# The reciprocal of two pairs in the slot of an existing small tile (linear attention and a squared-ReLU feed-forward, one core)

## The chip, the cores and the metric

One NeuronCore of one Trainium2 chip. The metric is the device time of one execution in microseconds (us). A shorter time is better.

## The reference

Eight batches, eight heads, 576 positions, 64 channels per head. Every head goes through a linear attention, the eight heads are laid side by side to 512 channels, and the 4608 rows go through a feed-forward of width 2048:

```python
q_s = softmax(q, over the 64 channels)
k_s = softmax(k, over the 576 positions)
kv  = einsum('bhsd,bhse->bhde', k_s, v)
x   = einsum('bhsd,bhde->bhse', q_s, kv)      # then heads side by side: 4608 x 512
h   = x @ w_in                                # 512 x 2048
out = (relu(h) ** 2) @ w_out                  # 2048 x 512
```

## The kernel before

**Numbers.** Everything is float32. A large matrix product is made from three products of `float32r` operands: each operand is split into a high part and a low rest, and high by high, high by low and low by high are added up in one PSUM bank.

**Stages.** The rows are worked in blocks of 512 columns (one block per batch, and one block of the eight batches' last 64 positions). Blocks 0, 1 and 2 go through the feed-forward one by one: `h_part` (lines 894 to 899) multiplies a 128x128 piece of `wi[fc]` (stationary operand) with a 512-column piece of `x_hi` or `x_lo` (moving operand), 12 matmuls for each of 16 chunks `fc`; `relu`, `square`, `g_high` and `g_low` make `g_hi` and `g_lo`; `out_part` multiplies pieces of them (stationary) with the 512 columns of `wo[fc]` (moving), 12 matmuls a chunk. Blocks 0 and 2 read `x_hi0` and `x_lo0`, block 1 reads `x_hi1` and `x_lo1`. The other six blocks are worked in three steps of two blocks with a Strassen-like scheme, seven products for eight: `product` multiplies a piece of a weight tile `wp` (stationary) with 512 columns of `xh_...` or `xl_...` (moving), and `out_unit` multiplies a piece of `g` (stationary) with the 512 columns of `wp`, `wo` or `wo_back` (moving). Attention of later batches runs between the matmuls of earlier blocks.

**Order.** Two lists written by hand, `ORDER` and `LIST`, give the order of all units; `InOrder` ties each instruction to the one before it on its engine, so that every engine issues in just that order. SyncE issues nearly all DMAs, also in that order. What an instruction waits for follows from the tiles that it reads and writes.

**The reciprocals.** `kv` of a pair of heads has 128 rows and a 65th column with the sum that the rows are divided by. `rs` adds 1e-9 to that column and `rr` takes the reciprocal, on VectorE, into a tile `rs` of 128x1 with the tag `rs0` or `rs1`. From batch 2 on, two pairs are taken together (`joint`): there `kr` does the same for two columns at once in a tile `rsj` of 128x2 with a tag of its own, and multiplies with it into `kf`.

**Where tiles lie.** SBUF is laid out by pool in the order `const`, `work`, `attn`, `weights`, `stay`, and behind them `first` and later `late`; within a pool, tags lie in the order in which they are first used, each slot rounded up to 32 bytes. Adding up the sizes (the first tile of `const` starts at byte 1152 of a partition) gives these starts:

| tiles | pool | first byte | modulo 64 |
|---|---|---|---|
| `x_hi0`, `x_lo0`; in the same slots later `g` | const | 1152, 9344 | 0 |
| a tile of 352 bytes that nothing uses (`pad_back`) | const | 37152 | 32 |
| `r`, `w_sum`, `c`, `g_hi`, `g_lo` | work | 37504 to 47744, 2048 apart | 0 |
| `mc0`, `mc1`, `rs0`, `rs1` | attn | 61056, 61088, 61120, 61152 | 0, 32, 0, 32 |
| `rsj`, the last tile of its pool | attn | 63104 | 0 |
| `w`, `a`, `T`, `tb`, `xf`, `o`, `left` | weights | 63136 to 76960 | 32 |
| `wi`, `wo`, `wp`, `xh_...`, `xl_...`, `far` | stay | 79520 and on, 4096 apart | 32 |
| `x_hi1`, `x_lo1`; in the same slots later `wo_back`; `kvs` | late | 210592, 218784, 226976 | 32 |

The pieces that a matmul reads of these tiles begin a multiple of 512 bytes behind the tile's start, so a piece has the tile's remainder modulo 64.

Of the kernel before, what the change touches and what calls it, by code (L numbers as in the profile page):

```python
# [8 lines left out]
F32 = mybir.dt.float32  # L9
# [7 lines left out]
P = 128  # L17
# [10 lines left out]
NB = 2  # L28
# [281 lines left out]
def attention_ffn_kernel(ctx: ExitStack, tc: tile.TileContext, q, k, v, w_in, w_out, out):  # L310
# [14 lines left out]
    attn_pool = ctx.enter_context(tc.tile_pool(name="attn", bufs=1))  # L325
# [23 lines left out]
    def next_bank(who):  # L349
        if who == "z":  # L350
            return rest[2]
        n = taken[who]
        taken[who] += 1
        return rest[n % 2 + (0 if who == "h" else 2)]
# [12 lines left out]
    for tag in ("m0", "m1"):  # L367
        attn_pool.tile([P, 2, D], F32, name=tag, tag=tag)
    for tag in ("mc0", "mc1", "rs0", "rs1"):
        attn_pool.tile([P, 1], F32, name=tag, tag=tag)  # L370

    v0 = [t.rearrange("p h j d -> p (h j d)")[:, : 2 * LOW * D].rearrange("p (h j d) -> p h j d", h=2, j=LOW) for t in vt]

# [93 lines left out]
    def pair_units(b, pr):  # L467
        n = b * NPAIR + pr
        i = n % NB
# [4 lines left out]
        s = {}  # L474
# [64 lines left out]
            e.pool.memset(vt[pr][:, :, :, D:], 1.0)  # L539

        def rs():
            s["rs"] = attn_pool.tile([P, 1], F32, name="rs", tag=f"rs{i}")
            e.dve.tensor_scalar_add(s["rs"], s["kv"][:, D : D + 1], 1e-9)

        def rr():
# [46 lines left out]
        for f in (  # L592
            kmax, T, mc, spread, ke, kexp, qm, qsub, qexp, qs, qadd, rc, qmul, kv, padv, rs, rr, kvn_,
            qt4, cp, qt1, cps, at, xhi, xlo, atl, left, XL,
        ):
            units[f"{f.__name__.rstrip('_')}{b}{pr}"] = f

    def attention(b, pr, two):
        n = b * NPAIR + pr
        kk, qq, vv = tiles(b, pr)  # L600
        st = {"v": vv}
# [92 lines left out]
                    )  # L694

        def rs():
            st["rs"] = attn_pool.tile([P, 1], F32, name="rs", tag=f"rs{n % NB}")
            e.dve.tensor_scalar_add(st["rs"], st["kv"][:, D : D + 1], 1e-9)

        def rr():  # L700
# [114 lines left out]
        def keep_raw():  # L815
            e.sp.dma_start(x_raw[b][pr // 2][:, pr % 2], st["xr"])

        fine = dict(Bw=bounce_out, B=bounce_in, rs=rs, rr=rr, kf=kf, kh=kv_high, kl=kv_low)
        fine.update(
            kmax=lambda: (k_max(), k_rows(), k_spread()), ke=k_sub, kexp=k_exp, qsub=lambda: (q_max(), q_less()),  # L820
            qexp=q_exp, qn=lambda: (q_sum(), q_scale(), q_turn()), kv=kv, qh=q_high, ql=q_low,
        )
        micro = dict(
            km=k_max, k1=k_rows, k2=k_spread, ke=k_sub, kx=k_exp, qm=q_max, qd=q_less, qx=q_exp, qs=q_sum, qy=q_scale,
            tb=q_turn, Bw=bounce_out, B=bounce_in, kp=k_pad, kr=lambda: (rs(), rr(), kf()),
            kh=kv_high, kl=kv_low, XL=keep_left, XR=keep_raw, kvat=kv, st=st,
            kv=lambda: kv(next_bank("z" if b > THREE[-1] else "a")[:, : D + 1]),
# [22 lines left out]
    def joint(b, pr):  # L850
        sts = [pairs[b, pr + i]["st"] for i in range(NB)]
        st = {}

        def kv():
            ps = st["kv"] = next_bank("z" if b > THREE[-1] else "a")[:, : NB * P].rearrange("p (i f) -> p i f", i=NB)
            for i in range(NB):
                pairs[b, pr + i]["kvat"](ps[:, i, : D + 1])

        def kr():
            rs = attn_pool.tile([P, NB, 1], F32, name="rsj", tag="rsj")  # L860
            e.dve.tensor_scalar_add(rs, st["kv"][:, :, D : D + 1], 1e-9)
            e.dve.reciprocal(rs, rs)
            st["kf"] = attn_pool.tile([P, NB, D], F32, name="kf", tag="kf0")
            e.dve.tensor_tensor(st["kf"], st["kv"][:, :, :D], rs.broadcast_to([P, NB, D]), op=ALU.mult)

        def kz():
            z = kv_split[0].bitcast(F32)
            if b in THREE:
                e.pool.memset(z[HALF:, :, :, :D], 0.0)
                e.pool.memset(z[:HALF, :, :, D:], 0.0)  # L870
            else:
                e.pool.memset(z[HALF:, :, 0, D:], 0.0)
                e.pool.memset(z[:HALF, :, 1, D:], 0.0)

        def kh():
            kvs, kf = kv_split[0], st["kf"]
            for h in range(2):
                e.act.copy(kvs[half[h], :, 0, half[h]] if b in THREE else kvs[half[h], :, h, :D], kf[half[h]])
            if b not in THREE:
                for h in range(2):  # L880
                    e.act.copy(kvs[half[1 - h], :, h, :D], kf[half[h]])

        def kl():
            kvs, kf = kv_split[0], st["kf"]
            for h in range(2):
                own = half[h]
                lo, hi = (kvs[own, :, 1, own], kvs[own, :, 0, own]) if b in THREE else (
                    kvs[own, :, h, D:], kvs[own, :, h, :D]
                )
                e.dve.tensor_tensor(lo, kf[own], hi.bitcast(F32), op=ALU.subtract)  # L890

        return dict(kv=kv, kr=kr, kz=kz, kh=kh, kl=kl)

    def h_part(ps, blk, fc, cc):
# [78 lines left out]
    for j in range(NPR + 1):  # L973
        for p in PAIR if j < NPR else TAIL:
            i = j - (p in ("S4", "o1"))
# [261 lines left out]
    for token in ORDER:  # L1237
        name, _, bank = token.partition(":")
# [98 lines left out]
```

## Time and profile before

| | |
|---|---|
| median of 3 runs | 851.17 us (850.32 to 852.03) |
| the profiled execution | 850.77 us, span in the profile 849.0 us |
| TensorE busy | 840.7 us, 99% of the span |
| VectorE, ScalarE, GpSimd busy | 538.4, 487.2, 288.1 us |
| granted TensorE clock, mean over the span | 1.00 |

The span runs from the first to the last instruction in the trace; the profiled execution's own time is 1.77 us longer. PE is TensorE's matmul, PEld its load of the stationary operand, DVE VectorE, ACT ScalarE, POOL GpSimd, SP SyncE. All of the kernel's instructions are recorded by one helper and so bear one line number, L290; they are told apart by the tiles (`out<-in`, buffer numbers left out). A matmul's duration in the trace overlaps with that of the next one; how fast a row of matmuls goes is read from the starts: the start of one group less the start of the group before it, divided by the number of matmuls in the latter. Below, this is called the pitch.

### The profile page before, as it was taken

What the parts mean: (1) busy time and instruction counts of PE and PEld (TensorE: products, weight loads), DVE (VectorE), ACT (ScalarE), POOL (GpSimd) and SP (SyncE); (2) the same over time, 40 slices, a digit from 0 to 9 for tenths busy, and PEclk for the clock granted to TensorE, in tenths of its full rate; (3) what the DMA queues carried; (4) which work ended last, traced back from release to release, by engine and by line L of the source; (5) the groups of instructions that cost most, each with busy time, mean ns of one, the idle gap of its engine ahead of it and who ended that gap; (6) DMA issues with size and microseconds to landing.
All of it is one profiled execution on the core that took longest, in us unless ns stands there. A gap on an engine that the chain in (4) does not pass through costs nothing.

```text
span 849.0 us, 12969 instructions
## 1 busy us (share of the span) xinstructions
PE 840.7 (99%) x4286; PEld 678.0 (80%) x4286; DVE 538.4 (63%) x1098; ACT 487.2 (57%) x898; POOL 288.1 (34%) x269
## 2 busy tenths in 40 slices
PE   8999999999999999999999999999999999999997
PEld 6777788888888887888888878888888788888886
DVE  7898888778787779857677787553257132222421
ACT  4888866667556656676567455565473144444411
POOL 4578654466657546242323252211004000000000
PEclk9999999999999999999999999999999999999999
DMA  9969987963787889989889847866575275554611
GB/s 239 277 184 298 278 281 223 311 196 103 220 263 225 234 264 268 277 271 252 239 245 265 258 140 213 266 188 179 170 237 170 93 225 162 155 169 152 178 48 49
DMA packets 156594, 179.65 MB, mean 212 GB/s; under 512 B 51696, under 2 KB 120304, under 8 KB 156528
## 3 DMA queue, kind: packets, MB, share of 16 engines
q1 hardware_dynamic: 155776, 177.88, 70.6%
q10 hardware_dynamic: 752, 0.95, 0.4%
q8 instruction: 34, 0.56, 0.3%
q14 instruction: 32, 0.26, 0.1%
HBM read 133.69 MB, written 45.09 MB: 211 GB/s over the span
## 4 chain that ended last, share of the span: by engine, by line
PE 90%; DVE 3%; DMA 3%; issue 1%; SPq 1%; ACT 1%; POOL 1%; DVEq 0%; POOLq 0%; ACTq 0%
PE bank L290 90%; DMA raw_o<-in_moe_w_out_dram 1%; DVE m L290 1%; DMA qt<-in_q_dram 1%; DMA kt<-in_k_dram 1%; SPq L290 1%; DMA raw_i<-in_moe_w_in_dram 0%; POOL qs L290 0%; DVE g_lo L290 0%; DVE bank L290 0%; DVE w L290 0%; DVE ke L290 0%; DVE xf L290 0%; DVE qs L290 0%; DVE qm L290 0%
## 5 line engine op out<-in xcount | busy, mean ns | idle before, releaser
L290 PE MATMUL bank<-wp,g 128*128 128x512 f32 x648 | 164.7, 395 | 0.0
L290 PEld LDWEIGHTS bank<-wp,g 128*128 128x128 f32 x648 | 120.5, 187 | 28.6
L290 PE MATMUL bank<-x_hi,wi 128*128 128x512 f32 x384 | 132.9, 400 | 0.0
L290 PE MATMUL bank<-xh_T,wp 128*128 128x512 f32 x384 | 131.4, 392 | 0.0
L290 PE MATMUL bank<-wo,g_hi 128*128 128x512 f32 x384 | 122.3, 399 | 0.0
L290 PE MATMUL bank<-xh_B,wp 128*128 128x512 f32 x288 | 98.4, 392 | 0.0
L290 POOL TENSOR_TENSOR qs<-qT,qs 64x640 fp32r<-64x640 f32 (+1 forms) x40 | 64.2, 1606 | 95.1 <-ACT qs L290 66.1
L290 DVE TENSOR_TENSOR c<-c,bank 128x512 f32<-128x512 f32 x48 | 32.9, 686 | 89.5 <-ACT c L290 89.1
L290 PEld LDWEIGHTS bank<-x_hi,wi 128*128 128x128 f32 x384 | 72.2, 188 | 17.2 <-issue 0.5
L290 PEld LDWEIGHTS bank<-xh_T,wp 128*128 128x128 f32 x384 | 72.1, 188 | 17.0 <-ACT bank L290 1.2
L290 ACT ACTIVATE far<-far 128x512 f32<-128x512 f32 x96 | 60.7, 632 | 40.3 <-DVE far L290 39.0
L290 PEld LDWEIGHTS bank<-wo,g_hi 128*128 128x128 f32 x384 | 70.5, 188 | 16.6 <-issue 0.7
L290 PE MATMUL bank<-wo,g_lo 128*128 128x512 f32 x192 | 75.8, 395 | 0.0
L290 PE MATMUL bank<-x_lo,wi 128*128 128x512 f32 x192 | 75.5, 393 | 0.0
L290 PE MATMUL bank<-xl_T,wp 128*128 128x512 f32 x192 | 74.7, 389 | 0.0
L290 PE MATMUL bank<-wo_back,g 128*128 128x512 f32 x288 | 73.2, 395 | 0.0
L290 DVE TENSOR_TENSOR far<-far,bank 128x512 f32<-128x512 f32 x48 | 32.9, 686 | 50.4 <-PE bank L290 50.3
L290 DVE TENSOR_TENSOR g<-far,g 128x512 fp32r<-128x512 f32 x48 | 33.9, 745 | 48.2 <-ACT g L290 48.1
L290 PEld LDWEIGHTS bank<-wo_back,g 128*128 128x128 f32 x288 | 53.6, 187 | 12.7
L290 PEld LDWEIGHTS bank<-xh_B,wp 128*128 128x128 f32 x288 | 54.1, 188 | 11.7
L290 POOL TENSOR_TENSOR qn<-qn,qs 128x640 f32<-128x640 f32 x30 | 37.8, 1262 | 72.4 <-DVE qs L290 56.2
L290 ACT CAST g<-far 128x512 fp32r<-128x512 f32 x48 | 27.6, 620 | 54.1 <-PE bank L290 53.9
(138 smaller groups left out, 1525.3 us busy)
## 6 DMA issues: line engine op xcount, KB each, us to landing
wp<-w_outs SPq DMA_DIRECT2D x54, 512.0 KB, 4.4
wp<-w_sums SPq DMA_DIRECT2D x96, 256.0 KB, 3.7
wp<-w_own SPq DMA_DIRECT2D x72, 256.0 KB, 3.5
out_dram<-o SPq DMA_DIRECT2D x68, 128.0 KB, 2.8
raw_i<-in_moe_w_in_dram SPq DMA_DIRECT2D x16, 512.0 KB, 6.6
raw_o<-in_moe_w_out_dram SPq DMA_DIRECT2D x16, 512.0 KB, 6.8
bounce<-tb SPq DMA_DIRECT2D x24, 320.0 KB, 3.4
qT<-bounce SPq DMA_DIRECT2D x96, 80.0 KB, 3.0
```

What stands on the lines that cost most here:

```text
L290: ins = f(*args, **kwargs)
```

## The change

The tile `rsj` is gone. `kr` takes the tag `rs0`, whose slot now has room for two columns; the single reciprocals `rs` take the first column of a tile of that size. All instructions, their order and their shapes stay as they were. A slot of 8 bytes is rounded up to 32 like one of 4, so `rs0` and `rs1` keep their places and sizes; the slot of `rsj` at the end of the pool `attn` is no longer there, and everything in `weights`, `stay`, `first` and `late` starts 32 bytes lower.

```diff
     for tag in ("mc0", "mc1", "rs0", "rs1"):
-        attn_pool.tile([P, 1], F32, name=tag, tag=tag)
+        attn_pool.tile([P, NB if tag[0] == "r" else 1], F32, name=tag, tag=tag)
...
         def rs():
-            s["rs"] = attn_pool.tile([P, 1], F32, name="rs", tag=f"rs{i}")
+            s["rs"] = attn_pool.tile([P, NB], F32, name="rs", tag=f"rs{i}")[:, :1]
             e.dve.tensor_scalar_add(s["rs"], s["kv"][:, D : D + 1], 1e-9)
...
         def rs():
-            st["rs"] = attn_pool.tile([P, 1], F32, name="rs", tag=f"rs{n % NB}")
+            st["rs"] = attn_pool.tile([P, NB], F32, name="rs", tag=f"rs{n % NB}")[:, :1]
             e.dve.tensor_scalar_add(st["rs"], st["kv"][:, D : D + 1], 1e-9)
...
         def kr():
-            rs = attn_pool.tile([P, NB, 1], F32, name="rsj", tag="rsj")
+            rs = attn_pool.tile([P, NB], F32, name="rs", tag="rs0").rearrange("p (i o) -> p i o", o=1)
             e.dve.tensor_scalar_add(rs, st["kv"][:, :, D : D + 1], 1e-9)
             e.dve.reciprocal(rs, rs)
```

## Rows read from the trace of the kernel before

**Rows 1.** Page: span, and busy time of TensorE.

```profile
span 849.0 us, 12969 instructions
PE 840.7 (99%) x4286; PEld 678.0 (80%) x4286; DVE 538.4 (63%) x1098; ACT 487.2 (57%) x898; POOL 288.1 (34%) x269
```

**Rows 2.** Chain in order of time: start us, length us, what.

```profile
46.49 116.16 PE bank L290 x591
...
162.73 0.60 ACT g_hi L290
...
195.48 648.72 PE bank L290 x3178
```

**Rows 3.** Tile rsj: duration ns min/median/max, first and last start us.

```profile
L290 DVE RECIPROCAL rsj<-rsj x11: 165/166/167, 173.9 to 561.7; 128x2 f32<-128x2 f32 x11
```

**Rows 4.** Timeline of TensorE at 700 us: start us, length us, what.

```profile
701.31 2.96 PE L290 MATMUL bank<-wp,g 128*128 128x512 f32 x12
704.11 0.39 PE L290 MATMUL bank<-xh_B,wp 128*128 128x512 f32 x1
...
706.60 0.40 PE L290 MATMUL bank<-xh_B,wp 128*128 128x512 f32 x1
706.84 0.86 PE L290 MATMUL bank<-wo_back,g 128*128 128x512 f32 x3
```

**Rows 5.** Groups on the page: the load of the stationary operand.

```profile
L290 PEld LDWEIGHTS bank<-wp,g 128*128 128x128 f32 x648 | 120.5, 187 | 28.6
```

**Rows 6.** Timeline of TensorE from 805 us.

```profile
804.84 2.96 PE L290 MATMUL bank<-wp,g 128*128 128x512 f32 x12
...
841.24 2.95 PE L290 MATMUL bank<-wp,g 128*128 128x512 f32 x12
```

**Rows 7.** Timeline of TensorE: a chunk of block 1, then one of block 2.

```profile
212.87 0.40 PE L290 MATMUL bank<-x_hi,wi 128*128 128x512 f32 x1
...
215.63 0.63 PE L290 MATMUL bank<-wo,g_hi 128*128 128x512 f32 x2
...
294.74 0.40 PE L290 MATMUL bank<-x_hi,wi 128*128 128x512 f32 x1
...
297.54 0.60 PE L290 MATMUL bank<-qs,kvs 128*128 128x320 f32 x3
```

**Rows 8.** Timeline of TensorE: warm-up matmuls (two looks, which overlap).

```profile
6.15 3.82 PE L290 MATMUL bank<-x_hi 128*128 128x512 f32 x16
...
8.22 1.52 PE L290 MATMUL bank<-x_hi 128*128 128x512 f32 x6
```

**Rows 9.** Windows: busy PE, PEld, DVE, ACT, POOL (instructions), PE clock, DMA share, GB/s.

```profile
7.10:9.50 2.40, 2.40 (x12) 2.00 (x11) 2.33 (x3) 0.85 (x2) 2.26 (x2) 1.00 1.05 292
325.00:450.00 125.00, 125.00 (x654) 101.96 (x653) 93.50 (x218) 83.46 (x152) 46.55 (x37) 1.00 0.90 257
450.00:849.00 399.00, 394.19 (x1781) 319.54 (x1779) 178.27 (x315) 184.81 (x323) 45.06 (x33) 1.00 0.57 174
805.00:840.00 35.00, 35.00 (x151) 28.11 (x151) 7.76 (x12) 6.88 (x12) 0.00 (x0) 1.00 0.13 42
```

**Rows 10.** Windows, TensorE alone, by tile: wi, g_hi, g_lo, g, wp; last g again.

```profile
46.49:849.00 802.51, 132.67 (x525) 1.00 0.70 209
46.49:849.00 802.51, 122.29 (x384) 1.00 0.70 209
46.49:849.00 802.51, 75.80 (x192) 1.00 0.70 209
46.49:849.00 802.51, 286.21 (x1152) 1.00 0.70 209
46.49:849.00 802.51, 397.19 (x1656) 1.00 0.70 209
450.00:849.00 399.00, 243.52 (x990) 1.00 0.57 174
```

**Rows 11.** Waits of SyncE's DMA queue: us in total, times, longest us.

```profile
SPq L290 <- PE bank L290: 218.7, 120, 5.2
```

## The prediction

> **What bounds the kernel now.** I read the page first. TensorE is busy for 99% of the span [rows 1], so the next view is the chain of waits in order of time: two pieces on TensorE hold 116.16 and 648.72 us of the 849.0 us, and only the first 46.5 us and the stretch from 162.73 to 195.48 us run over other engines and loads [rows 2]. Even there TensorE is hardly ever without work. A change that leaves every instruction and its order alone can then matter in one way: by what one matmul takes. So the third view is TensorE's timeline, and what to take from it is the pitch, not the printed length of a matmul (0.39 or 0.40 us, which overlaps with the next).
>
> Near 700 us the pitch has two levels. Twelve matmuls with `wp` stationary and `xh_B` or `xl_B` moving run from 704.11 to 706.84 us: 2.73 us / 12 = 227.5 ns. The twelve before them, with `g` stationary and `wp` moving, run from 701.31 to 704.11 us: 2.80 / 12 = 233.3 ns [rows 4]. All have 512 columns of float32r, at a granted clock of 1.00, its 2.4 GHz level [rows 9]. The load of the next stationary operand (187 ns [rows 5]) runs beside the matmul before it, so each matmul has two reads of SBUF under way: its moving columns and the next stationary piece.
>
> What tells the two kinds apart in the table of addresses: `wp` and `xh_B` both start at 32 modulo 64, while `g` starts at 0 and `wp` at 32. I test this reading in three places:
> - Traffic does not make it. From 804.84 to 841.24 us thirteen chunks of 12 with `g` stationary take 36.40 us / 156 = 233.3 ns [rows 6], though DMA is at 0.13 and GpSimd idle there [rows 9]. Near 700 us, with far more going on, it is the same number.
> - The same code at another address differs. A chunk `h` of block 1 (moving `x_hi1` at 32, stationary `wi` at 32) takes 215.63 - 212.87 = 2.76 us / 12 = 230.0 ns; one of block 2 (moving `x_hi0` at 0, stationary `wi` at 32) takes 297.54 - 294.74 = 2.80 / 12 = 233.3 ns [rows 7].
> - Only the warm-up has both operands at 0 (both are `x_hi0`): sixteen matmuls from 6.15 us have 3.82 less the 0.39 of the last = 3.43 us / 15 = 228.7 ns, and the last six 1.13 / 5 = 226 ns [rows 8], while DMA is at 1.05 of its engines and VectorE busy nearly throughout [rows 9].
>
> So I read: **unequal remainders modulo 64 cost 233.3 ns, equal ones about 227.5.** The rows speak of 64 only because no pair differs otherwise.
>
> **The change part by part.**
> - *The slot.* The table's last tile of `attn` (32 bytes) goes, so `weights`, `stay` and `late` go from 32 to 0 modulo 64, while `const` and `work` stay at 0. All large matmuls then have both operands at 0.
> - *kr.* The same add, reciprocal (165 ns [rows 3]) and multiply on the same shapes: 0. Sharing `rs0` could add a wait on its earlier readers. Those on ScalarE belong to batches 0 and 1 and come before every joint in the order; later ones are on VectorE, as `kr` itself. Should one wait appear, the copies `kvs` stand behind it, and VectorE's own slack (538.4 of 849.0 us busy [rows 1]) covers it.
> - *Matmuls that go from unequal to equal remainders.* From 46.49 us on: 384 with `g_hi`, 192 with `g_lo`, 1152 with `g`, and of 525 with `wi` all but block 1's 16 x 12 = 192, so 333 [rows 10]. Together 2061.
>   - The 1152 of the three steps: 1152 x (233.3 - 227.5) = 6.7 us.
>   - The other 909 lie before 325 us, where equal pairs run at 230.0 (block 1) rather than 227.5. Bounds: 909 x 3.3 = 3.0 and 909 x 5.8 = 5.3 us; I take 4.1, the middle, since the warm-up's 228.7 lies between the two.
> - *Matmuls that stay equal* (from 32 and 32 to 0 and 0): 1656 - 648 = 1008 products [rows 5, 10] and block 1's 192. I take 0. Upper bound on the cost if 0 and 0 means the 228.7 of the warm-up's sixteen: 1008 x 1.2 = 1.2 us.
> - *The first 46.5 us*: the chain there runs over loads and VectorE, 0.
> - *162.73 to 195.48 us*: the chain is not on TensorE; a faster TensorE waits for ScalarE, VectorE and GpSimd instead. Its share of the gain, 32.75 / 802.5 x 10.8 = 0.4 us, I take off.
> - *Transfers into moved tiles.* No row has one transfer at both addresses. SyncE's queue waited 218.7 us for TensorE [rows 11], so refills follow TensorE rather than lead it: 0 from both sides, within the range.
>
> Sum: 6.7 + 4.1 - 0.4 = 10.4 us. The profiled execution's 850.77 us become 840.4 (span 838.6); the median shown is 0.4 above it, so **840.8 us**. What ends last stays TensorE. Next in line is DMA at 0.90 between 325 and 450 us [rows 9].
>
> The far ends: all 2061 at 226 ns give 2061 x 7.3 = 15.0 us, so 836.2. All large matmuls at 228.7 give 2061 x 4.6 - 1.2 = 8.3 us, so 842.9.
>
> **A rule against it.** The rows show the pitch of one matmul to go with the addresses of two operands [rows 4, 7]. The Trainium skill, "TensorE: Matmul & The Clock Gate", section "Step-by-step: what each phase is for", says that TensorE has two independent read ports in SBUF and that loading the next weights takes no read bandwidth from the running matmul. By that rule an address could not matter and the time would stay at 851.2. The trace speaks against it with 230.0 beside 233.3 ns for one line of code.
>
> **The rivals.**
> 1. *The pitch belongs to the role, not the address* (`g` as stationary operand, banks that change every three matmuls), or the slot is not given back and nothing moves. For it: the long runs of `g` are all at 233.3 and there is none with `g` at another address. Against it: block 1 against block 2 [rows 7]. Time: 851.2.
> 2. *Slower: a start at 0 modulo 64 is itself what costs.* Every slow pair has one operand at 0, and every fast pair of the two-operand kinds has both at 32; so it could be the 0, not the inequality. Then the 2061 gain nothing, and the 1008 products go from 227.5 to 233.3 (+5.8 us) and block 1 from 230.0 to 233.3 (+0.6): 857.6. It decides at the products' pitch. Only the warm-up speaks against it, with 228.7 and 226 ns for 0 and 0; but there both operands begin at the same byte, which no other pair does.
> 3. *The gain is given back where others are close.* With DMA at 0.90 of its engines between 325 and 450 us and VectorE at 93.50 of 125 us [rows 9], TensorE could wait there instead. If only what lies behind 450 us comes through, 990 x 5.8 = 5.7 us [rows 10]: 845.4. Against it: the queue waits for TensorE, not the reverse [rows 11].
>
> **How the numbers follow.** About 0.2% (1.7 us) is what a measurement of this kernel can tell from no change. Forecast 0.74, rival 3 0.08, rival 1 0.09, rival 2 0.09. Rivals 1 and 2 are the same and the slower case; the forecast and rival 3 are both faster by more than 0.2%: 0.82. The range 837.5 to 846.5 takes in the forecast with the bounds of its 909 (minus 1.1, plus 1.2), most of the way to the 226 ns end, the 842.9 of the other end, and rival 3; it leaves out rivals 1 and 2, 0.18.
>
> **What would show it.** Right: groups with `g` stationary start 2.73 us apart per 12 instead of 2.80; block 2's chunks come down to block 1's; products stay at 2.73; counts and clock are unchanged; the chain's last piece is shorter by some 9 us. Wrong: products at 2.80 (rival 2), `g` groups still at 2.80 (rival 1), or new idle time of TensorE ended by DMA or ScalarE between 325 and 450 us (rival 3).

## The result and the profile after

The changed kernel takes **838.71 us** in the median of 4 runs (838.34 to 840.46), the kernel before, measured beside it, 851.06 us (850.32 to 852.03): a ratio of 0.9858, 95% interval 0.9841 to 0.9875, so 12.4 us or 1.4% faster. The forecast was 840.8 us, in a range of 837.5 to 846.5. One of the ten executions of experiment 5 took 1387.65 us at a granted clock of 0.557; its ratio leaves that one out.

All engines issue the same instructions in the same order. The page's head, against [rows 1]:

```profile
span 837.1 us, 12969 instructions
PE 828.8 (99%) x4286; PEld 678.2 (81%) x4286; DVE 540.8 (65%) x1098; ACT 486.7 (58%) x898; POOL 288.2 (34%) x269
```

The span is 11.9 us shorter and TensorE is busy for 11.9 us less, with the same 4286 matmuls; no other engine's busy time moved by more than 2.4 us. The last long piece of the chain of waits (start us, length us, what), against [rows 2]:

```profile
194.58 637.71 PE bank L290 x3178
```

It holds the same 3178 matmuls as before and is 648.72 - 637.71 = 11.0 us shorter; it begins 195.48 - 194.58 = 0.9 us earlier. Nearly all of the gain lies there. TensorE's timeline near the same work as in [rows 4]:

```profile
692.03 2.88 PE L290 MATMUL bank<-wp,g 128*128 128x512 f32 x12
694.75 0.39 PE L290 MATMUL bank<-xh_B,wp 128*128 128x512 f32 x1
...
697.47 0.84 PE L290 MATMUL bank<-wo_back,g 128*128 128x512 f32 x3
```

The twelve with `g` now take 2.72 us, 226.7 ns each (233.3 before), and the twelve products 2.72 us as well (2.73 before): the two kinds are at one pitch. The long run at the end, against [rows 6], and a chunk of block 1 and one of block 2, against [rows 7]:

```profile
791.31 2.88 PE L290 MATMUL bank<-wo_back,g 128*128 128x512 f32 x12
...
829.39 2.88 PE L290 MATMUL bank<-wp,g 128*128 128x512 f32 x12
```

```profile
211.74 0.39 PE L290 MATMUL bank<-x_hi,wi 128*128 128x512 f32 x1
...
214.46 0.61 PE L290 MATMUL bank<-wo,g_hi 128*128 128x512 f32 x2
...
291.96 0.39 PE L290 MATMUL bank<-x_hi,wi 128*128 128x512 f32 x1
...
294.68 0.60 PE L290 MATMUL bank<-qs,kvs 128*128 128x320 f32 x3
```

Fourteen chunks of 12 at the end take 829.39 - 791.31 = 38.08 us, 226.7 ns each. Both blocks' chunks take 2.72 us; before, block 2's took 2.80 and block 1's 2.76. The reciprocal did not change: the 21 on tile `rs`, 11 of them with two columns, take 163 to 167 ns, where those of `rsj` took 165 to 167 [rows 3].

SyncE's queue still waits for TensorE, 203.4 us in 120 waits [rows 11].

### The profile page after: what moved, and what is told of

Read it like the earlier page. It is cut to its first block, busy times and chain, and to the rows that moved or that the text cites. A ratio compares the mean times of both kernels' runs of the same rounds, so it can differ in the third digit from the quotient of the medians.

```text
span 837.1 us, 12969 instructions
## 1 busy us (share of the span) xinstructions
PE 828.8 (99%) x4286; PEld 678.2 (81%) x4286; DVE 540.8 (65%) x1098; ACT 486.7 (58%) x898; POOL 288.2 (34%) x269
## 4 chain that ended last, share of the span: by engine, by line
PE 90%; DVE 4%; DMA 2%; issue 1%; POOL 1%; ACT 1%; SPq 1%; DVEq 0%; POOLq 0%; ACTq 0%
PE bank L290 90%; DVE m L290 1%; DMA raw_o<-in_moe_w_out_dram 1%; DMA qt<-in_q_dram 1%; SPq L290 1%; DMA raw_i<-in_moe_w_in_dram 0%; POOL qs L290 0%; DVE qs L290 0%; DVE g_lo L290 0%; DVE w L290 0%; POOL qn L290 0%; DVE xf L290 0%; DVE bank L290 0%; DVE r L290 0%; DVE qm L290 0%
## 5 line engine op out<-in xcount | busy, mean ns | idle before, releaser
L290 PE MATMUL bank<-wp,g 128*128 128x512 f32 x648 | 160.7, 390 | 0.0
L290 PE MATMUL bank<-wo,g_hi 128*128 128x512 f32 x384 | 120.3, 394 | 0.0
L290 PE MATMUL bank<-wo_back,g 128*128 128x512 f32 x288 | 71.4, 389 | 0.0
L290 DVE TENSOR_TENSOR g<-far,g 128x512 fp32r<-128x512 f32 x48 | 35.7, 781 | 43.5 <-ACT g L290 43.4
```

What stands on the lines that cost most here:

```text
L290: ins = f(*args, **kwargs)
```

## The experiments

Times are medians; ratios are to the kernel before on the same chip. The experiments ran on three chips; the kernel before took 850.70 us in experiments 2 to 4, 850.34 in 5 to 7 and 850.35 in 9 and 10, against 851.06 beside the changed kernel. So a difference from the changed kernel's 838.71 us is known to about 1 us. Addresses are quoted as the distance of the moving operand from the stationary one.

**1. The pitch by itself.** A kernel of its own: groups of 48 matmuls with slices of one tile `mv` and one tile `st`, both of which start at 128 modulo 256 (the sizes ahead of them added up from byte 1152).

```diff
+    def one(n, m, s):
+        pe.matmul(banks[n % 8], st[:, s // 4 : s // 4 + P], mv[:, m // 4 : m // 4 + NT], start=True, stop=True)
...
+    for n, (m, s) in enumerate(PAIRS):
+        for _ in range(GROUP):
+            one(n, m, s)
+    for i in range(GROUP):
+        one(n, 32 * (i % 2), 32 * (i % 2))
+    for i in range(GROUP):
+        one(n + 1, 32 * (i % 2), 32 * (1 - i % 2))
```

> This kernel leaves the whole computation out and writes one matmul's result to all of the output: it measures the pitch alone. Groups of 48 matmuls (128x128 stationary, 512 moving columns, float32r), each group into its own bank, with the moving and the stationary operand starting at chosen bytes from a multiple of 512. Theory (unequal remainders modulo 64 are what costs, and the read that collides with the moving columns is the load of the NEXT stationary piece): 0/0, 32/32, 0/64, 0/128 and 0/256 bytes at about 226.7 ns, 0/32, 32/0 and 0/96 at about 233.3 ns; distances other than 0 or 32 were never seen, so 4 to 60 bytes are open between these two levels. Of the two alternating groups, the one whose own operands are equal but whose next stationary piece is unequal is at 233, and the one whose own operands are unequal but whose next stationary piece is equal is at 227. Rival 1 (own pair counts, not the next load): the two alternating groups the other way round, 227 and 233. Rival 2 (role, banks or traffic, not the address): every group at the same pitch. Rival 3 (the modulus is 512, not 64): 0/64, 0/128 and 0/256 at 233.

Its timeline on TensorE (start us, length us; a group's pitch is the next group's start less its own, by 48), and one window over all groups (busy PE, PEld, ACT, POOL, then clock, DMA share, GB/s):

```profile
29.70 11.05 PE L31 MATMUL bank_a<-mv,st 128*128 128x512 f32 x48
40.59 11.36 PE L31 MATMUL bank_b<-mv,st 128*128 128x512 f32 x48
51.79 11.36 PE L31 MATMUL bank_c<-mv,st 128*128 128x512 f32 x48
...
151.98 11.36 PE L31 MATMUL bank_d<-mv,st 128*128 128x512 f32 x48
163.18 11.40 PE L31 MATMUL bank_e<-mv,st 128*128 128x512 f32 x48
...
185.57 11.05 PE L31 MATMUL bank_g<-mv,st 128*128 128x512 f32 x48
196.46 11.28 PE L31 MATMUL bank_h<-mv,st 128*128 128x512 f32 x48
...
252.42 11.28 PE L31 MATMUL bank_e<-mv,st 128*128 128x512 f32 x48
263.54 11.22 PE L31 MATMUL bank_f<-mv,st 128*128 128x512 f32 x48
274.60 11.05 PE L31 MATMUL bank_g<-mv,st 128*128 128x512 f32 x48
```

```profile
29.70:285.65 255.95, 255.95 (x1105) 207.42 (x1103) 0.00 (x0) 0.00 (x0) 1.00 0.00 1
```

| moving / stationary, bytes | pitch, ns | | moving / stationary, bytes | pitch, ns |
|---|---|---|---|---|
| 0/0 (40.59 - 29.70 = 10.89 us) | 226.9 | | 0/256 | 226.9 |
| 0/32 | 233.3 | | 16/0 | 231.5 |
| 32/0 | 233.3 | | 16/16 | 231.3 |
| 32/32 | 227.3 | | 4/4 | 237.7 |
| 0/4 | 232.9 | | starts 0 and 32 by turns: | |
| 0/64 | 233.3 | | own pair equal, next piece unequal | 231.7 |
| 0/96 | 234.0 | | own pair unequal, next piece equal | 230.4 |
| 0/128 | 232.5 | | | |

The eight pairs that are not in the table lie between 230.0 (0/24) and 233.3 ns.

Three things follow. Where the two operands start does it, with nothing else running on the core: rival 2 falls. **But the modulus is not 64: 0/64 and 0/128 are as slow as 0/32, and only 0/256 is fast again**; here theory and rival 3 each got a part wrong. And equality is not enough: 16/16 and 4/4 are slow although equal; of equal pairs, those at multiples of 32 bytes were fast, and all tiles of the kernel start at one. Neither order of the alternating groups came out as expected: both lie between the levels, so this run does not tell which load it is, nor that it is a load.

**2. The move alone.** The changed kernel, with 32 bytes put back where `rsj` stood; `kr` still shares `rs0`.

```diff
+    w_pool.tile([P, 8], F32, name="ahead", tag="ahead", bufs=1)
```

> The changed kernel with an unused tile of 32 bytes in front of the pool weights: kr still uses the slot of rs0, but everything from weights on lies again where it lay in the kernel before. Theory (the move alone makes the time): the kernel before's time, 851.1 us, ratio 1.000, groups with g stationary at 2.80 us per 12. Rival (the shared slot, its waits or kr itself make it): the changed kernel's time, 838.7 us, ratio 0.9858.

Measured: 851.33 us, ratio 1.000 (0.9981 to 1.0019). Timeline:

```profile
700.81 2.96 PE L290 MATMUL bank<-wp,g 128*128 128x512 f32 x12
703.60 0.39 PE L290 MATMUL bank<-xh_B,wp 128*128 128x512 f32 x1
```

2.79 us per 12 and the whole gain gone: the shared slot and `kr` bring nothing.

**3. 64 bytes instead of 32**, at the same place as in run 2.

```diff
+    w_pool.tile([P, 16], F32, name="ahead", tag="ahead", bufs=1)
```

> The changed kernel with an unused tile of 64 bytes at the same place: weights, stay and late lie 32 bytes higher than in the kernel before and 64 higher than in the changed one. Theory (remainder modulo 64): the changed kernel's time, 838.7 us, ratio 0.986. Rival (a modulus of 128 or more, or just the place that the changed kernel happens to have): 851 us, or between the two.

Measured: 846.38 us in the median (844.17 in the execution shown), ratio 0.9945 (0.993 to 0.996), between the two, which the rival allowed for and the theory did not. Timeline:

```profile
696.40 2.91 PE L290 MATMUL bank<-wp,g 128*128 128x512 f32 x12
699.14 0.39 PE L290 MATMUL bank<-xh_B,wp 128*128 128x512 f32 x1
```

A third level: 2.74 us / 12 = 228.3 ns with the moving `wp` 64 bytes above `g`. Modulo 64 the operands are equal and the time is still 7.7 us above the changed kernel's, so the remainder modulo 64 is not the rule.

**4. Everything 32 bytes higher**, distances unchanged.

```diff
+    const.tile([P, 8], F32, name="ahead", tag="ahead")
     x_hi = [const.tile([P, NCC, NT], F32R, name="x_hi0", tag="x_hi0")]
```

> The changed kernel with an unused tile of 32 bytes in front of the first tile of const: every tile of the kernel lies 32 bytes higher, so all large operands start at 32 modulo 64 and stay equal to each other. Theory (only the difference of the two operands counts): 838.7 us, ratio 0.986, 2.72 us per 12 everywhere. Rival (a start at 0 modulo 64 is what the changed kernel gained, for matmuls, transfers or the other engines): all 3300 large matmuls at 233 ns, so 851 us or, with the products slower too, about 858 us, ratio 1.00 to 1.008.

Measured: 840.75 us (838.15 to 841.83), ratio 0.988 (0.9861 to 0.9899). Timeline, and the chain of waits from 196 us on:

```profile
694.80 2.88 PE L290 MATMUL bank<-wp,g 128*128 128x512 f32 x12
697.52 0.39 PE L290 MATMUL bank<-xh_B,wp 128*128 128x512 f32 x1
```

```profile
196.34 121.47 PE bank L290 x721
...
326.61 5.94 DMA qT<-bounce
...
340.93 494.13 PE bank L290 x2359
```

2.72 us per 12 with both operands at 32 modulo 64. So a start at 0 is no gain in itself, and the rival falls. The median is 2.0 us above the changed kernel's. The execution shown (841.83 us) is the longest of the four: its chain comes to TensorE at 196.34 us instead of 194.58 and leaves it again from 317.81 to 340.93, for SyncE's queue, a load and other engines. From 310 to 345 us TensorE was busy for 34.36 of 35.00 us, in the changed kernel for all 35.00. So a little of the gain can be lost there, which is rival 3 of the prediction on a small scale. Why, and in how many executions, is open.

**5. Only const 32 bytes higher.** The unused tile behind `const` gives the 32 bytes back, so `work` and all behind it stay.

```diff
-PAD = 88
+PAD = 80
...
+    const.tile([P, 8], F32, name="ahead", tag="ahead")
```

> The changed kernel with 32 bytes in front of const and the unused tile behind const 32 bytes smaller: only x_hi0, x_lo0 and the g tiles of the three steps (and the small tiles of const) lie 32 bytes higher; work, weights, stay and late stay. So 1152 matmuls with g and 333 of blocks 0 and 2 have unequal operands again, the 576 with g_hi and g_lo stay equal. Theory (the distance of the two operands, as in the runs so far: 233.2 ns against 227.4): 1485 x 5.8 = 8.6 us more than the changed kernel, 847.3 us, ratio about 0.995. Rival (the moved tiles of stay and weights make the gain, whatever const does): 838.7 us, ratio 0.986.

Measured: 848.94 us, ratio 0.9984 (0.9974 to 0.9994), so 10.2 us above the changed kernel where 8.6 were expected.

The matmuls with `g`, then the products with `xh_T` (window on TensorE and its length, busy us, count, then clock, DMA share, GB/s):

```profile
46.97:847.20 800.23, 285.57 (x1152) 1.00 0.69 209
46.97:847.20 800.23, 131.83 (x384) 1.00 0.69 209
```

Near 700 us twelve with `g` take 702.22 - 699.43 = 2.79 us again although `wp` did not move: the rival falls. 10.2 us / 1485 = 6.9 ns looks like one price for each unequal matmul, but it is not: the 1152 with `g` are busy for 285.57 - 279.10 = 6.5 us more than in the changed kernel, 5.6 ns each, and the 384 products with `xh_T`, none of whose operands moved, for 131.83 - 130.72 = 1.1 us more (the changed kernel's rows stand in the next section). Equal matmuls that run beside unequal ones lose a little too.

**6. Work 32 bytes higher, first try.**

```diff
-PAD = 88
+PAD = 96
...
+    w_pool.tile([P, 8], F32, name="ahead", tag="ahead", bufs=1)
```

> The changed kernel with work (and attn) 32 bytes higher, all else unmoved: only the 576 matmuls with g_hi and g_lo are unequal. Theory: 576 x 5.8 = 3.3 us more than the changed kernel, less what the stretch before 195 us swallows, so 841 to 842 us, ratio 0.988 to 0.990; together with the run before, the two parts add up to the whole change. Rival (the stretch before 195 us is bound by other engines): 838.7 to 839.5 us.

Measured: 845.16 us, ratio 0.9942 (0.9927 to 0.9957), neither of the two. The edit did not do what was said of it: both additions together put `weights`, `stay` and `late` 64 bytes higher against `const`, which is experiment 3's distance, and, with `work` another 32 bytes off, this run tells nothing on `work` alone. Run 9 mends it.

**7. 256 bytes less between const and the rest.**

```diff
-PAD = 88
+PAD = 24
```

> The changed kernel with the unused tile behind const 256 bytes smaller: work and all behind it lie 256 bytes lower against const, so x_hi0 with wi and g with wp differ by a multiple of 256 that is not one of 512. Theory as mended by the two runs before (equal modulo 256): 838.7 us, ratio 0.986. Rival (equal modulo 512): const's 1485 matmuls at 230 to 233 ns, 843 to 847 us, ratio 0.990 to 0.996.

Measured: 837.99 us (837.87 to 838.18), ratio 0.9852 (0.9838 to 0.9867). Modulo 256 is enough.

**8. More distances, and short runs.** As experiment 1 with other pairs; in three of the last runs the bank changes with every matmul, so that each has a row.

```diff
+    for r, pair in enumerate((
+        lambda i: (0, 32 * (i // 6 % 2)), lambda i: (32 * (i // 6 % 2), 0), lambda i: (32 * (i // 6 % 2),) * 2,
+        lambda i: (0, 32 * (i % 2)), lambda i: (32 * (i % 2), 0), lambda i: (0, 0),
+    )):
+        for i in range(GROUP):
+            one(n + r + (i if r < 3 else 0), *pair(i))
```

> Again the pitch alone, the whole computation left out. First, groups of 48 with the moving operand a distance above the stationary one: 0, 32, 64, 96, 128, 160, 192, 224, 256, 288, 320, 512 bytes. Theory (period 256, as 0/256 at 226.7 and 0/64 at 233.3 in the first such run and the full kernel with 64 bytes show): 0, 256 and 512 at 226.7; 32 and 288 at 233.3; 64 and 320 at 229 to 230; 192 and 224 at 233. Rival (period 512): 256 above 228 and 288 or 320 unlike 32 or 64. 96, 128 and 160 are open; below 226.7 anywhere would show that a better kernel exists than one with equal remainders. Then three runs of 48 in which the stationary operand, the moving one, or both change between 0 and 32 every six matmuls: if the load of the next stationary piece is what collides, the sixth matmul of each six (equal operands, next one unequal) is slow in the first run and the sixth of the unequal six is fast; if the own pair counts, the sixth goes like the five before it.

```profile
52.94 11.16 PE L31 MATMUL bank_c<-mv,st 128*128 128x512 f32 x48
63.94 11.37 PE L31 MATMUL bank_d<-mv,st 128*128 128x512 f32 x48
...
130.85 11.37 PE L31 MATMUL bank_b<-mv,st 128*128 128x512 f32 x48
142.06 11.16 PE L31 MATMUL bank_c<-mv,st 128*128 128x512 f32 x48
153.06 11.07 PE L31 MATMUL bank_d<-mv,st 128*128 128x512 f32 x48
...
185.88 11.36 PE L31 MATMUL bank_g<-mv,st 128*128 128x512 f32 x48
197.07 11.06 PE L31 MATMUL bank_h<-mv,st 128*128 128x512 f32 x48
...
241.21 11.42 PE L31 MATMUL bank_d<-mv,st 128*128 128x512 f32 x48
252.47 11.21 PE L31 MATMUL bank_e<-mv,st 128*128 128x512 f32 x48
263.52 11.05 PE L31 MATMUL bank_f<-mv,st 128*128 128x512 f32 x48
```

The rows shown are distances 64 and 96, then 288, 320 and 512, then the pairs 0/192 and 0/512, then three runs told of below. By the starts: 0 and 256 at 226.7 ns, 512 at 227.1; 32 and 288 at 233.5; 64 and 320 at 229.2; 96 at 233.5, 128 at 233.1, 160 at 234.2, 192 at 233.3 and 224 at 233.1. So the pitches at 0, 32 and 64 come back 256 bytes further on, and nothing lies below 226.7: no pair tried beats equal remainders. Four more pairs: 64/64 at 227.7, 96/32 at 229.0, 0/512 at 227.1, **and 0/192 at 197.07 - 185.88 = 11.19 us / 48 = 233.1 ns, although it is a distance of 64 modulo 256 like 64/0, 320/0 and 96/32, which take 229**. So equal remainders modulo 256 are the fast case wherever they were tried at multiples of 32, but what an unequal pair costs does not go by the distance modulo 256 alone.

In the run whose stationary piece changes every six (moving operand always at 0), the end of a first six and of the second:

```profile
209.11 0.40 PE L31 MATMUL bank_f<-mv,st 128*128 128x512 f32 x1
209.34 0.39 PE L31 MATMUL bank_g<-mv,st 128*128 128x512 f32 x1
...
210.50 0.40 PE L31 MATMUL bank_d<-mv,st 128*128 128x512 f32 x1
```

The sixth equal matmul (209.11, its next piece unequal) has the long form of 0.40 us where the five before it have 0.39; as it would if the load of the next piece, which runs beside it, is what collides. But the sixth unequal one (210.50, its next piece equal) is at 0.40 too, and the first two unequal ones (209.34 and 209.57) are at 0.39, which speaks against that. So does the run with the moving operand fixed at 0 and the stationary one at 0 and 32 by turns: by either reading half of its matmuls should be fast, but its pitch is 11.26 us / 48 = 234.6 ns, slower than unequal throughout. With the stationary one fixed and the moving one changing it is 11.05 / 48 = 230.2, midway, as either reading has it. How the two reads get in each other's way, and whether it is the two reads, stays open.

**9. Work alone, mended.**

```diff
-PAD = 88
+PAD = 32
...
+    w_pool.tile([P, 56], F32, name="ahead", tag="ahead", bufs=1)
```

> Mends the run with work 32 bytes higher, in which everything behind work came to lie 64 bytes higher as well. Here the unused tile behind const is 224 bytes smaller (work lies at 32 modulo 256 against const) and an unused tile of 224 bytes in front of weights brings weights, stay and late back to where the changed kernel has them. Only the 576 matmuls with g_hi and g_lo are unequal. Theory (equal modulo 256 is fast; unequal costs 5.8 ns and slows the equal ones next to it by a little): 576 x 5.8 = 3.3 us, of which what lies before 195 us comes through only in part (there the changed kernel gained 0.9 us where 441 x 5.9 = 2.6 were due), so 840.5 to 842.5 us, ratio 0.988 to 0.990. Rival (that stretch is bound by TensorE after all, with neighbours slowed too): 843 us or more.

Measured: 841.58 us (841.35 to 842.48), ratio 0.9898 (0.9882 to 0.9915): 2.9 us above the changed kernel, as expected. A chunk with `g_hi` and `g_lo`, and the chunk with `wi` behind it:

```profile
209.82 0.62 PE L290 MATMUL bank<-wo,g_hi 128*128 128x512 f32 x2
...
212.61 0.39 PE L290 MATMUL bank<-x_hi,wi 128*128 128x512 f32 x1
...
215.34 0.62 PE L290 MATMUL bank<-wo,g_hi 128*128 128x512 f32 x2
```

2.79 us for the first twelve, 2.73 for the second. Const's part (10.2) and work's part (2.9) add up to 13.1 us, the whole change to 12.4, each known to about 1 us.

**10. The kernel before, with equal distances.** `rsj` keeps its own slot; the distances are mended elsewhere.

```diff
-PAD = 88
+PAD = 24
...
+    w_pool.tile([P, 56], F32, name="ahead", tag="ahead", bufs=1)
```

> The kernel before, with rsj in its own slot and kr untouched; the unused tile behind const is 256 bytes smaller and an unused tile of 224 bytes stands in front of weights, so that const, work, stay and late are equal modulo 256, at other bytes than in the changed kernel. Theory (only the distance of the operands counts): the changed kernel's time, 838 to 839 us, ratio 0.985 to 0.987. Rival (the shared slot of the reciprocal is part of the gain): above 840 us, up to 851.

By the sizes only `work` and `attn` lie at other bytes than in the changed kernel, 256 lower; `weights`, `stay` and `late` lie where it has them (63136 - 256 + 224 = 63104).

Measured: 839.05 us (838.33 to 840.81), ratio 0.987 (0.9855 to 0.9885): the changed kernel's time without the change of slot. With experiment 2 this closes the question from both sides: the same `kr` at the old distance is slow, the old `kr` at the new distance is fast.

## Why the prediction was right, point by point

- **The bound and the mechanism held.** TensorE's pitch is what changed, it goes by where the two operands start against each other, and the kernel follows it almost fully. The prediction claimed no more than that; what inside the chip makes the pitch go by it, no run shows.
- **"Unequal remainders modulo 64" was wrong in its modulus.** Before, every unequal pair differed by 32 or by a multiple of 512 more or less, as the step itself said, so the rows could not tell 64 from 256. Experiments 1, 3, 7 and 8 put it at 256. That it made no difference here is luck: this change brings `const`, `work`, `stay` and `late` to one remainder modulo 512, while a move to a distance of 64 bytes, as good by the step, took 846.38 us (experiment 3).
- **The terms of the sum** can be read from the busy time of TensorE by tile. The changed kernel's rows for `wi`, `g_hi`, `g_lo` and `g`, against [rows 10]:

```profile
46.79:837.10 790.31, 130.67 (x525) 1.00 0.71 212
46.79:837.10 790.31, 120.25 (x384) 1.00 0.71 212
46.79:837.10 790.31, 75.01 (x192) 1.00 0.71 212
46.79:837.10 790.31, 279.10 (x1152) 1.00 0.71 212
```

- **The 1152 with `g`**: priced at 233.3 - 227.5 = 5.8 ns, so 6.7 us. They brought 286.21 - 279.10 = 7.1 us, 6.2 ns each: 0.4 too low. The fast level in the long runs is 226.7 and not 227.5.
- **The other 909**: 4.1 us, the middle between 3.0 and 5.3. With block 1's 192, `wi` brought 2.0 us, `g_hi` 2.0 and `g_lo` 0.8, together 4.8: 0.7 too low, and inside the bounds. (Some 24 of the matmuls with `g_hi` and `g_lo` lie behind 325 us, not before it.) The lower end rested on block 1's 230.0 ns, and that was one chunk. Another chunk of block 1 in the same trace takes 159.91 - 157.18 = 2.73 us, 227.5 ns:

```profile
157.18 0.39 PE L290 MATMUL bank<-x_hi,wi 128*128 128x512 f32 x1
...
159.91 0.63 PE L290 MATMUL bank<-wo,g_hi 128*128 128x512 f32 x2
```

  Both chunks have unequal ones on either side, and in the changed kernel the chunk of 230.0 takes 226.7. What made that one chunk slower than the other is open.
- **What stays equal**: taken as 0. This was the term with the largest error. The rows for `xh_T`, before and after:

```profile
46.49:849.00 802.51, 131.38 (x384) 1.00 0.70 209
46.79:837.10 790.31, 130.72 (x384) 1.00 0.71 212
```

  They fell by 0.7 us, those of `xh_B` by 0.4 (98.38 to 97.95), and those of `xl_B` and `xl_T` rose by 0.2 together: 0.9 us in all. Their distance did not change, but the matmuls beside them did; experiment 5 shows the same from the other side.
- **The stretch that TensorE does not bound**: 0.4 us taken off for 162.73 to 195.48 us. From the first long piece on TensorE to its last one (before, then after):

```profile
46.49:195.48 148.99, 148.93 (x770) 1.00 0.81 246
46.79:194.58 147.79, 147.41 (x771) 1.00 0.81 248
```

  The stretch begins 0.3 us later, and in it TensorE is idle for 0.38 us instead of 0.06. So about 0.6 us went there.
- **The sum.** The tiles together give 7.1 + 4.8 + 0.9 = 12.8 us and TensorE's busy time fell by 11.9, so 0.9 us was not kept (matmuls of different tiles overlap in the trace, so this remainder is rough). The terms were 0.4 + 0.7 + 0.9 us too low and the loss 0.5 too small; that leaves the 1.5 us between the forecast gain of 10.4 and the 11.9 by which the span fell. The errors are small and of one sign but for the last.
- **The rule of two independent read ports.** By the Trainium skill ("TensorE: Matmul & The Clock Gate", section "Step-by-step: what each phase is for") loading the next weights takes no SBUF read bandwidth from the running matmul. Read as the prediction read it, the operands' places could not matter; here the pitch is 226.9 ns at one distance and 233.3 at another, with no other engine at work (experiment 1), and the measurement decides. That it is the load which is in the way is not shown.
- **The rivals.** Role or bank (rival 1): against it stand experiments 1 and 2. A start at 0 as the cost (rival 2): against it, 226.7 ns for products now at 0. The gain given back where others are close (rival 3) did not happen in the changed kernel: its chain stays on TensorE from 194.58 us to the end of the matmuls. In the executions shown of experiments 4 and 10 a little of it did: their chains leave TensorE once more and come back at 340.93 and 338.90 us, and TensorE was idle for 0.6 and 0.3 us between 310 and 345 us.

## What to carry to other kernels

Read the pitch of matmuls from their starts, and by kind: two kinds of equal shape at two pitches are a finding, even at 99% TensorE. Take more than one chunk for a price: block 1 had 2.76 and 2.73 us in one trace. Where float32r matmuls of 512 columns follow one another, lay their moving and stationary tiles at the same remainder modulo 256 bytes, at multiples of 32, and look at it again whenever a small tile comes or goes ahead of them: 32 bytes were worth 1.4% here. When distances are moved in an experiment, work out every tile's new place first; experiment 6 was lost to a sum of two shifts.

## What the runs showed of the hardware that was not expected

- The pitch of back-to-back float32r matmuls (128x128 by 512) goes by where the two operands start: 226.7 to 227.7 ns where they are equal modulo 256 bytes and at multiples of 32, 229.0 to 229.2 with the moving operand 64 or 320 above, 232.5 to 234.2 at the other multiples of 32 tried (experiments 1 and 8). It is not symmetric, 64 below (0/64) being at 233.3, and 0/192 at 233.1 shows that the distance modulo 256 does not settle an unequal pair's pitch.
- Equal starts off a multiple of 32 are slow too: 231.3 ns at 16/16, 237.7 at 4/4, the slowest pair seen.
- What runs beside a matmul counts. Groups that change operands with every matmul lie at 231.7, 230.4 (experiment 1), 234.6 and 230.2 ns (experiment 8), where equal throughout is 226.7 and unequal throughout 233.3; a price for the own and one for the next stationary piece do not fit all four. In the full kernel 384 equal products take 130.72 us beside equal matmuls and 131.83 beside unequal ones (experiment 5).
